# One score pass per unit, a block-diagonal product for the last keys, and one shared pool of PSUM banks in a top-k attention kernel with a feed-forward block

## The chip, the cores and the metric

The kernel runs on one core of a Trainium2 chip. The metric is the device time of one execution in microseconds (us). The kernel before took 1854.19 us, the median of three runs (1853.1 to 1854.46). One more execution was profiled; it took 1853.37 us, and the span from its first to its last instruction is 1851.6 us. Five engines work beside each other: TensorE (PE, with its weight loads shown apart as PEld), VectorE (DVE), ScalarE (ACT), GpSimd (POOL) and SyncE (SP), which issues the transfers.

## The reference

There are 8 batches of 8 heads with 576 positions of 64 numbers. Per head, the scores of all queries against all keys are made, only the 32 largest scores of each query are kept, and a softmax over them weighs the values. The heads are then laid side by side into rows of 512 numbers, and a normalised feed-forward block with a residual follows.

```python
scores = scale * np.matmul(q, k.transpose(0, 1, 3, 2))
kth = np.partition(scores, -top_k, axis=-1)[..., -top_k:-top_k + 1]
scores = np.where(scores >= kth, scores, -1000000000.0)
attn = softmax(scores)                       # over the keys
x = heads_side_by_side(attn @ v)             # (8, 576, 512)
xn = (x - mean(x)) / sqrt(var(x) + 1e-6) * g_ln
out = x + np.maximum(xn @ w_ch1, 0.0) @ w_ch2
```

All inputs come as 64-bit or 32-bit floats, and the kernel computes in 32-bit floats. The feed-forward weights come as 64-bit numbers; the kernel fetches them in 32 pieces and turns them into 32-bit floats itself (class `Piece`).

## The kernel before, in words

**Jobs, units, groups.** A job is a batch and a pair of heads. A unit is one tile of 128 queries of both heads of a job, so it has two score tiles of 128 x 576. A job has four such units and a fifth, the rest unit, whose 64 last queries of both heads share one tile. In batch 0 a job is split in two, so that the first rows are finished early. There are 160 units. Two or three units form a group (`lo_half`, `hi_half`), over which the product with the values is made at once.

**The pipeline.** The main loop (lines 745 to 834) has one step per unit, and the order on each engine is the order in which the code is written. In step n, VectorE searches the 32 largest scores of unit n (`select`, four rounds of MAX8 and MATCH_REPLACE8, lines 358 to 375). TensorE makes the scores of unit n+1 (`scores`), ScalarE copies them from PSUM to `sc`, GpSimd masks unit n-1 (`mask`), ScalarE takes the exponential of unit n-2 (`weigh`), TensorE turns these weights so that keys lie on partitions (`turn`), and for the group whose last unit is n-3, `values` multiplies them with the values and `place` turns the product back and puts it into the rows `x`. `sc` has three buffers, `e` has two.

**The scores.** `scores(u, s)` (lines 330 to 356) makes half s of the keys, 288 columns, for both heads. A head has 64 numbers, so the product of the first head uses rows 0 to 63 of the array and that of the second rows 64 to 127. The two products go to two PSUM banks and are copied by two ScalarE instructions (line 356). The first half is written at the step's start (line 760), the second half behind the first turned tile (line 793).

**The values.** `values(g)` (lines 469 to 484) adds five pairs of products in one bank. In the first four, the values of each head (128 keys, 64 numbers) fill half of the array's columns. In the fifth, the last 64 keys of each head take one quarter of the array each. The number of columns that stream through is 256 for a group of two units and 320 with a rest unit.

**PSUM.** The eight banks are shared out at lines 101 to 103: two for the scores (`scps`), three for turned tiles (`tpps`), three for products (`mmps`: values, turned-back rows `xo`, both feed-forward products and the means of the weights).

**The feed-forward block.** When a batch's rows are finished its block is handed to a list (`give`, line 718), and `fill()`, called eight times in a step, takes products from it by a plan of costs and shares, so each step has a fixed number of feed-forward products at fixed places. A block of four row tiles stands for 20 steps. What is left at the end runs behind the loop. After batches 3 and 7 the block of the collected rest rows comes on top. While the weights are still being converted (the first 18 steps or so), `weights(n, phase)` puts that work between the parts of a step; `mean_of` (line 200) multiplies freshly converted weights on TensorE and is written at a step's end.

Of the kernel before, what the change touches and what calls it, by code (L numbers as in the profile page):

```python
# [11 lines left out]
FP32 = mybir.dt.float32  # L12
U32 = mybir.dt.uint32
PSUM = bass.MemoryType.PSUM
# [6 lines left out]
J = 4  # L21
# [7 lines left out]
def kernel(  # L29
# [34 lines left out]
    nc = tc.nc  # L64
    P = nc.NUM_PARTITIONS
    B, H, S, D = q.shape
# [4 lines left out]
    R = S - JP  # L71
# [6 lines left out]
    def pool(name, bufs, **kw):  # L78
        return ctx.enter_context(tc.tile_pool(name=name, bufs=bufs, **kw))

    GQ = 2 * P + R
    HALF = S // 2

    consts = pool("consts", 1)
    ldpool = pool("ld", 1)
    kqpool = pool("kq", 4)
    vpool = pool("v", 3)
    scpool = pool("sc", 3)
    wpool = pool("wk", 2)
    epool = pool("e", 2)  # L90
# [7 lines left out]
    opool = pool("o", 2)  # L98
    xtpool = pool("xt", 1)
    hpool = pool("h", NF + 2)  # L100
    scps = pool("scps", 2, space=PSUM)
    tpps = pool("tpps", 3, space=PSUM)
    mmps = pool("mmps", 3, space=PSUM)

    def const(shape, name):
        return consts.tile(shape, FP32, tag=name, name=name)

    def turned():
        return tpps.tile([P, 512], FP32, tag="tp", name="tp")

    def product(name):
        return mmps.tile([P, 512], FP32, tag="mm", name=name)

    ident = const([P, P], "ident")
    make_identity(nc, ident[:])
    eps = const([P, 1], "eps")
# [174 lines left out]
            job.ins[name] = t  # L291

    def load_values(job):
        vb = vpool.tile([P, 2 * J + 1, D], FP32, tag="v", name="vb")
        for hh in range(2):
            rows = v[job.b, 2 * job.hp + hh]
            k0, end = (0, JP) if hh == 0 else (R, 0)
            nc.sync.dma_start(
                vb[:, hh * J : (hh + 1) * J, :],
                rows[k0 : k0 + JP, :].rearrange("(c p) d -> p c d", p=P),  # L300
            )
            nc.sync.dma_start(
                vb[hh * R : (hh + 1) * R, 2 * J, :], rows[end : end + R, :]
            )
        job.v = vb

    def turn_heads(job):
        job.T = {}
        for name in "kq":
            job.T[name] = kqpool.tile([P, S], FP32, tag=name + "T", name=name + "T")  # L310
            nc.vector.transpose(job.T[name][:], job.ins[name][:])

    class Unit:
        def __init__(self, job, group, qt):
            self.job, self.group, self.qt = job, group, qt
            self.rest = qt == J
            self.tiles = [(0, 1)] if self.rest else [(0,), (1,)]
            self.sc = None  # L320
            self.shared = False

    class Group:
# [3 lines left out]
            self.units = [Unit(job, self, qt) for qt in qts]  # L327
            self.pt = self.den = None

    def scores(u, s):  # L330

        T = (u.job.twin or u.job).T
        kT, qT = T["k"], T["q"]
        q0 = u.qt * P
        ql = R if u.rest else P
        if u.sc is None:
            u.sc = scpool.tile([P, 2, S], FP32, tag="sc", name="sc")
        pss = [scps.tile([P, 512], FP32, tag="scps", name="scps") for _ in u.tiles]
        for ps, hs in zip(pss, u.tiles):
            for i, hh in enumerate(hs):  # L340
                r = slice(hh * D, (hh + 1) * D)
                parts = [(0, s * HALF, HALF)]
                if u.rest and hh == 1:
                    parts = [(0, R + s * HALF, HALF - s * R)]
                    if s:
                        parts += [(HALF - R, 0, R)]
                for o, k0, width in parts:
                    nc.tensor.matmul(  # L348
                        ps[i * R : i * R + ql, o : o + width],
                        qT[r, q0 : q0 + ql],  # L350
                        kT[r, k0 : k0 + width],
                        start=True,
                        stop=True,
                    )
        for t, ps in enumerate(pss):
            nc.scalar.copy(u.sc[:, t, s * HALF : (s + 1) * HALF], ps[:, 0:HALF])  # L356

    def select(u, i):

# [51 lines left out]
    def turn(u):  # L411

        g = u.group
        if g.pt is None:
            g.pt = ptpool.tile([P, 2 * J + 1, GQ], FP32, tag="pt", name="pt")
        q0 = sum(P for x in g.qts if x < u.qt)
# [51 lines left out]

    def values(g):
        vb = g.job.v  # L470
        av = product("av")
        for c in range(J + 1):
            for h in range(2):
                rows = slice(h * R, (h + 1) * R) if c == J else slice(0, P)
                blk = 2 * J if c == J else h * J + c
                nc.tensor.matmul(  # L476
                    av[h * D : (h + 1) * D, 0 : g.nq],
                    vb[rows, blk, :],
                    g.pt[rows, blk, 0 : g.nq],
                    start=(c == 0),  # L480
                    stop=(c == J),
                )
        g.oT = otpool.tile([P, GQ], FP32, tag="oT", name="oT")
        nc.scalar.copy(g.oT[:, 0 : g.nq], av[:, 0 : g.nq])  # L484
# [9 lines left out]
    def place(g):  # L494

        b, hp = g.job.b, g.job.hp
        for i, qt in enumerate(g.qts):
            if qt == J:
                if b % 2 == 0:
                    oTr[hp] = restpool.tile([P, P], FP32, tag=f"oTr{hp}", name="oTr")  # L500
                r0 = R * (b % 2)
                nc.gpsimd.tensor_copy(
                    oTr[hp][:, r0 : r0 + R], g.oT[:, i * P : i * P + R]
                )
                continue
            if (b, qt) not in xs:
                pair = xpool.tile([P, 2, DM], FP32, tag="x", name="x")
                for j in range(2):
                    xs[b, qt // 2 * 2 + j] = pair[:, j]
            ps = product("xo")  # L510
            nc.tensor.transpose(ps[:, 0:P], g.oT[:, i * P : (i + 1) * P], ident[:])
            put(xs[b, qt], ps, hp * P, g.den, 2 * qt)

    def place_rest(b, hp):
        if hp == 0:
            rs[b // 2] = rpool.tile([P, DM], FP32, tag="r", name="r")[:]
        ps = product("xo")
        nc.tensor.transpose(ps[:, 0:P], oTr[hp][:], ident[:])
        put(rs[b // 2], ps, hp * P, dr[b // 2], 2 * hp)

# [109 lines left out]
    jobs = []  # L630
# [6 lines left out]
    units = []  # L637
# [60 lines left out]
    def at(i):  # L698
        return units[i] if 0 <= i < N else None
# [35 lines left out]
    weights(-2, 0)  # L735
    turn_heads(fresh[0])
    load(fresh[1], nc.sync)
    scores(units[0], 0)
    scores(units[0], 1)
    load_gain()  # L740
    load_values(jobs[0])
    weights(-1, 0)
    weights(-1, 2)
    recips = {}
    for n in range(END):
# [3 lines left out]
        u, nxt, mk, ex = at(n), at(n + 1), at(n - 1), at(n - 2)  # L749
        g = at(n - 3).group if at(n - 3) and at(n - 3).group.last == n - 3 else None  # L750
# [5 lines left out]

        if ex:
            weigh(ex, 0)
        if nxt:
            scores(nxt, 0)  # L760
        if u:
            select(u, 0)
        for den in recips.pop(n, []):
# [6 lines left out]
        if g:  # L770
            values(g)
# [18 lines left out]
        weights(n, 1)  # L790
        fill()
        if nxt:
            scores(nxt, 1)
        fill()
        if g:
            place(g)
# [27 lines left out]
        if g and g.job.hp == NHP - 1:  # L824
            for qt in g.qts:
                if qt < J:
                    blk, i = block_of[g.job.b, qt]
                    blk.stats(i, xs[g.job.b, qt])
        if late and late.job.hp == NHP - 1:
            r = late.job.b // 2  # L830
            blk, i = block_of["r", r]
# [36 lines left out]
```

## Time and profile before

| what | value |
|---|---|
| median of three runs | 1854.19 us |
| profiled execution's own time | 1853.37 us |
| its span | 1851.6 us |
| TensorE busy | 1709.7 us (92%) |
| VectorE busy | 1520.9 us (82%) |
| GpSimd busy | 1210.2 us (65%) |
| ScalarE busy | 942.3 us (51%) |
| mean granted TensorE clock | 0.966 |

Times in the rows below are us from the span's start unless marked ns. A busy share is a mean over stretches that differ much, so the rows give the stretches apart. TensorE's ends are modelled: a matmul's row lasts longer than the time until the next one can start, so the start-to-start distance is what a matmul costs. Every matmul on 32-bit floats has two records in the trace, except the transposes, which have one. A wait in square brackets is the idle time of the engine just before the row, with the one that ended it.

### The profile page before, as it was taken

The numbers are of one execution on the slowest core, as the hardware profiler recorded it, in microseconds if no ns is written. First come the engines' busy times: TensorE is split into PE (matmuls) and PEld (weight loads), VectorE is DVE, ScalarE is ACT, GpSimd is POOL, SyncE is SP. The second block draws the span as 40 slices with busy tenths as digits, with TensorE's granted clock in tenths as the row PEclk, the third lists the DMA queues.
The fourth block names the chain that finished last, engine by engine and source line by source line (L and its number), as shares of the span: only waits on it lengthen the run. The fifth ranks groups of instructions, "written<-read, shape, count | busy, mean of one in ns | idle before, by whom it ended". The sixth has DMA issues, their size and how long they took to land.

```text
span 1851.6 us, 22080 instructions
## 1 busy us (share of the span) xinstructions
PE 1709.7 (92%) x6849; PEld 827.4 (45%) x6849; DVE 1520.9 (82%) x3155; ACT 942.3 (51%) x2430; POOL 1210.2 (65%) x956
## 2 busy tenths in 40 slices
PE   3565998888999999999999999999999999999998
PEld 1223645533444444444444644444444444444455
DVE  7889899999999999999877688999999999960000
ACT  4566956544655465555444546545654565542110
POOL 5878877777777777677565557777777777760000
PEclk9676999999999999999999999999999999999999
DMA  7322221111111011111101011101110110000000
GB/s 185 91 81 64 59 38 24 23 18 26 21 22 24 22 26 20 20 31 31 20 19 25 19 31 20 20 19 32 32 20 19 31 23 16 6 12 6 6 18 11
DMA packets 210429, 57.16 MB, mean 31 GB/s; under 512 B 201604, under 2 KB 201608, under 8 KB 210312
## 3 DMA queue, kind: packets, MB, share of 16 engines
q1 hardware_dynamic: 207936, 55.46, 13.4%
q8 instruction: 54, 0.88, 0.2%
q10 hardware_dynamic: 2376, 0.30, 0.1%
q14 instruction: 63, 0.52, 0.1%
HBM read 46.27 MB, written 9.44 MB: 30 GB/s over the span
## 4 chain that ended last, share of the span: by engine, by line
PE 62%; DVE 14%; issue 11%; POOL 8%; ACT 5%; DMA 0%; POOLq 0%; SPq 0%; DVEq 0%; ACTq 0%
PE hps L574 20%; PE ops L591 19%; PE scps L348 8%; DVE m L366 7%; PE av L476 7%; DVE wk L371 6%; PE tp L421 5%; POOL e L396 2%; POOL w L175 1%; POOL size L174 1%; POOL e L399 1%; POOL e L394 1%; POOL size L165 1%; ACT xT L566 1%; ACT sc L356 1%
## 5 line engine op out<-in xcount | busy, mean ns | idle before, releaser
L396 POOL TENSOR_SCALAR e<-sc,m 128x576 f32<-128x576 f32 x270 | 599.0, 2218 | 287.2 <-PE tp L450 87.1
L366 DVE MAX8 m<-wk 128x8 f32<-128x576 f32 x864 | 612.9, 746 | 1.8
L574 PE MATMUL hps<-xT,w 128*128 128x512 f32 (+1 forms) x1408 | 574.8, 532 | 22.6 <-ACT xT L566 13.7
L591 PE MATMUL ops<-w,h 128*128 128x512 f32 x1152 | 565.2, 609 | 1.8 <-ACT x L488 1.2
L371 DVE MATCH_REPLACE8 wk<-m,wk 128x576 f32<-128x576 f32 x576 | 423.9, 743 | 0.0
L399 POOL TENSOR_TENSOR e<-e,sc 128x576 f32<-128x576 f32 x270 | 380.6, 1410 | 22.5
L356 ACT COPY sc<-scps 128x288 f32<-128x288 f32 x576 | 204.9, 403 | 249.5 <-PE scps L348 170.1
L574 PEld LDWEIGHTS hps<-xT,w 128*128 128x128 f32 x1408 | 241.5, 192 | 190.2 <-issue 147.3
L348 PE MATMUL scps<-kT,qT 64*128 64x288 f32 (+3 forms) x1344 | 255.7, 455 | 28.7 <-ACT sc L356 20.7
L591 PEld LDWEIGHTS ops<-w,h 128*128 128x128 f32 x1152 | 193.3, 191 | 183.8 <-issue 179.3
L366 DVE MAX8 m<-sc 128x8 f32<-128x576 f32 x288 | 203.6, 744 | 68.0 <-ACT sc L356 67.9
L406 ACT ACTIVATE e<-e,bias 128x576 f32<-128x576 f32 x288 | 224.9, 781 | 6.5 <-POOL e L399 5.8
L421 PE MATMUL tp<-ident,e 128*128 128x128 f32 x1152 | 183.3, 283 | 39.7 <-ACT e L406 36.2
L421 PEld LDWEIGHTS tp<-ident,e 128*128 128x128 f32 x1152 | 143.4, 145 | 167.8 <-issue 95.3
L371 DVE MATCH_REPLACE8 wk<-m,sc 128x576 f32<-128x576 f32 x288 | 212.0, 743 | 0.0
L348 PEld LDWEIGHTS scps<-kT,qT 64*128 64x128 f32 (+1 forms) x1344 | 107.3, 180 | 231.6 <-issue 72.3
L433 ACT COPY pt<-tp 128x512 f32<-128x512 f32 x256 | 151.0, 590 | 102.6 <-PE tp L421 101.1
L476 PE MATMUL av<-pt,vb 128*64 128x320 f32 (+3 forms) x1280 | 186.5, 426 | 3.9 <-ACT pt L433 2.4
L586 ACT ACTIVATE h<-hps 128x512 f32<-128x512 f32 (+1 forms) x176 | 92.2, 524 | 131.8 <-PE hps L574 131.5
L601 POOL TENSOR_TENSOR o<-o,x 128x512 f32<-128x512 f32 x32 | 40.8, 1274 | 178.4 <-ACT o L600 178.3
L476 PEld LDWEIGHTS av<-pt,vb 128*64 128x64 f32 (+1 forms) x1280 | 83.2, 139 | 113.5 <-issue 59.4
L484 ACT COPY oT<-av 128x256 f32<-128x256 f32 (+1 forms) x64 | 25.6, 400 | 136.5 <-PE av L476 136.4
(68 smaller groups left out, 959.3 us busy)
## 6 DMA issues: line engine op xcount, KB each, us to landing
raw<-in_moe_w_ch_dram SPq DMA_DIRECT2D x32, 512.0 KB, 3.9
kin<-in_k_dram SPq DMA_DIRECT2D x128, 72.0 KB, 2.4
vb<-in_v_dram SPq DMA_DIRECT2D x72, 128.0 KB, 2.5
qin<-in_q_dram SPq DMA_DIRECT2D x124, 72.0 KB, 2.4
out_dram<-o SPq DMA_DIRECT2D x32, 256.0 KB, 2.1
vb<-in_v_dram SPq DMA_DIRECT2D x72, 16.0 KB, 2.3
dr<-den SPq DMA_DIRECT2D x64, 0.2 KB, 1.7
out_dram<-o SPq DMA_DIRECT2D x8, 128.0 KB, 2.3
```

What stands on the lines that cost most here:

```text
L348: nc.tensor.matmul(ps[i * R : i * R + ql, o : o + width], qT[r, q0 : q0 + ql], kT[r, k0 : k0 + width], start=True, stop=True,)
L356: nc.scalar.copy(u.sc[:, t, s * HALF : (s + 1) * HALF], ps[:, 0:HALF])
L366: nc.vector.max(m[:, t, :], u.cur[t])
L371: nc.vector.match_replace(u.wk[t][:], m[:, t, :], u.cur[t], LOWEST)
L396: nc.gpsimd.tensor_scalar(e, sc, u.thr[:, t, 7:8], MASKED, ALU.is_lt, ALU.mult)
L399: nc.gpsimd.tensor_tensor(e, e, sc, ALU.add)
L406: nc.scalar.activation(u.e[:, t], u.e[:, t], AF.Exp, bias=u.bias[:, t : t + 1], scale=scale, accum_out=g.den[:, col : col + 1],)
L421: nc.tensor.transpose(ps[:, c * P : (c + 1) * P], u.e[:, t, c * P + t * R : (c + 1) * P + t * R], ident[:],)
L433: nc.scalar.copy(g.pt[:, t * J : (t + 1) * J, q0 : q0 + P], ps[:].rearrange("p (c n) -> p c n", n=P),)
L476: nc.tensor.matmul(av[h * D : (h + 1) * D, 0 : g.nq], vb[rows, blk, :], g.pt[rows, blk, 0 : g.nq], start=(c == 0), stop=(c == J),)
L574: nc.tensor.matmul(ps["h"][:, 0:N], w1[:, c, f * P : (f + 1) * P], xT[0][:, c, 0:N], start=(c == 0), stop=(c == NC - 1),)
L591: nc.tensor.matmul(ps["o"][:], hT[f][:, i * P : (i + 1) * P], w2[:, f, :], start=(f == 0), stop=(f == NF - 1),)
```

## The change

Three things change, and the costs and shares of the plan stay as they were.

**Scores in one go.** `scores(u)` makes both halves, four banks' worth, and then issues the four copies. It stands only where the second half stood; the call at the step's start is gone.

**Last keys as one product.** Three constant tiles of 128 x 128, `ends0` to `ends2`, are set to zero once by GpSimd. The transfers of the last 64 keys' values go into two diagonal blocks of one of them, so that one full product of 128 rows and 128 columns does what the fifth pair did. It is now the first product of the sum.

**Banks shared anew.** Scores, turned tiles, the values' product and `xo` take turns in one pool of five banks (`brief`). Three banks remain for the feed-forward products and the means.

```diff
-    scps = pool("scps", 2, space=PSUM)
-    tpps = pool("tpps", 3, space=PSUM)
+    psps = pool("ps", 5, space=PSUM)
     mmps = pool("mmps", 3, space=PSUM)
+    def brief(name):
+        return psps.tile([P, 512], FP32, tag="ps", name=name)
...
+    ends = [const([P, P], f"ends{i}") for i in range(NV)]
+    for t in ends:
+        nc.gpsimd.memset(t[:], 0.0)
...
             nc.sync.dma_start(
-                vb[hh * R : (hh + 1) * R, 2 * J, :], rows[end : end + R, :]
+                job.ends[hh * R : (hh + 1) * R, hh * D : (hh + 1) * D],
+                rows[end : end + R, :],
             )
...
-    def scores(u, s):
+    def scores(u):
+        u.sc = scpool.tile([P, 2, S], FP32, tag="sc", name="sc")
+        made = [score_half(u, s) for s in range(2)]
+        for s, pss in enumerate(made):
+            for t, ps in enumerate(pss):
+                nc.scalar.copy(u.sc[:, t, s * HALF : (s + 1) * HALF], ps[:, 0:HALF])
...
-        av = product("av")
-        for c in range(J + 1):
+        av = brief("av")
+        nc.tensor.matmul(
+            av[:, 0 : g.nq], g.job.ends[:], g.pt[:, 2 * J, 0 : g.nq],
+            start=True, stop=False,
+        )
+        for c in range(J):
             for h in range(2):
...
-        if nxt:
-            scores(nxt, 0)
         if u:
             select(u, 0)
...
         if nxt:
-            scores(nxt, 1)
+            scores(nxt)
```

On TensorE, in the step of a rest unit in a later batch, the order of before is this (scps are scores, av the values' product, tp turned weights, xo the turned-back product, ops a feed-forward product):

```order
L348 MATMUL scps<-kT,qT 128x288 x2
L476 MATMUL av<-pt,vb 64x256 x10
L421 MATMUL tp<-ident,e 128x128 x4
L348 MATMUL scps<-kT,qT 128x288 x2
L511 MATMUL xo<-ident,oT 128x128 x2
L591 MATMUL ops<-w_125,h 128x512
L421 MATMUL tp<-ident,e 128x128 x4
```

The same place in the changed kernel:

```order
L485 MATMUL av<-pt,ends_116 128x256
L491 MATMUL av<-pt,vb 64x256 x8
L434 MATMUL tp<-ident,e 128x128 x4
L362 MATMUL scps<-kT,qT 128x288 x4
L526 MATMUL xo<-ident,oT 128x128 x2
L606 MATMUL ops<-w_128,h 128x512
L434 MATMUL tp<-ident,e 128x128 x4
```

The two products at the step's start moved behind the first turned tile, and the two quarter products of the sum became one full product at its front.

On ScalarE, in the fourth step, while weights are converted, the order of before is this (sc_485 are the next unit's scores, e_500 the mask of the unit before, e_397 the weights of the unit before that):

```order
L406 ACTIVATE e_397,den_380<-e_397,bias_396 128x576
L356 COPY sc_485<-scps_486 128x288
L356 COPY sc_485<-scps_487 128x288
L384 ACTIVATE less_501<-m3_476 128x1
L385 ACTIVATE bias_499<-m0_389 128x2
L386 ACTIVATE e_500<-sc_303,less_501 128x576
```

The same place in the changed kernel:

```order
L419 ACTIVATE e_393,den_383<-e_393,bias_392 128x576
L397 ACTIVATE less_497<-m3_479 128x1
L398 ACTIVATE bias_495<-m0_385 128x2
L399 ACTIVATE e_496<-sc_343,less_497 128x576
L400 ACTIVATE e_496<-e_496 128x576
```

The two copies of scores no longer stand ahead of the four instructions that prepare the mask; they follow later in the step with the other two.

On TensorE, in the same fourth step, before:

```order
L204 MATMUL mean_479<-w1_124,gmat_179 128x512 x4
L348 MATMUL scps_486<-kT_427,qT_429 128x288
L348 MATMUL scps_487<-kT_427,qT_429 128x288
L421 MATMUL tp_519<-ident_117,e_397 128x128 x4
L348 MATMUL scps_536<-kT_427,qT_429 128x288
L348 MATMUL scps_537<-kT_427,qT_429 128x288
```

And in the changed kernel:

```order
L212 MATMUL mean_482<-w1_127,gmat_182 128x512 x4
L434 MATMUL tp_515<-ident_120,e_393 128x128 x4
L362 MATMUL scps_533<-kT_423,qT_425 128x288
L362 MATMUL scps_534<-kT_423,qT_425 128x288
L362 MATMUL scps_537<-kT_423,qT_425 128x288
L362 MATMUL scps_538<-kT_423,qT_425 128x288
```

The turned tile now comes straight behind the mean, and the four score products behind it.

## Rows read from the trace of the kernel before

**Rows 1.** Windows: stretch, length, busy of PE, PEld, DVE, ACT, POOL; clock, DMA.

```profile
0.00:200.00 200.00, 115.34 (x428) 58.58 (x429) 164.83 (x320) 127.01 (x302) 146.20 (x133) 0.76 0.40 102
200.00:500.00 300.00, 262.10 (x1205) 140.61 (x1204) 298.62 (x623) 176.66 (x485) 230.87 (x182) 0.95 0.13 28
500.00:875.00 375.00, 371.52 (x1535) 169.42 (x1534) 359.28 (x753) 200.75 (x524) 280.81 (x217) 1.00 0.13 25
875.00:1121.00 246.00, 243.77 (x980) 122.01 (x980) 186.48 (x386) 114.20 (x292) 143.78 (x109) 1.00 0.11 22
1121.00:1653.00 532.00, 526.66 (x2154) 239.10 (x2153) 506.94 (x1061) 289.74 (x758) 393.14 (x304) 1.00 0.11 21
1653.00:1852.00 199.00, 190.30 (x553) 97.72 (x551) 4.76 (x14) 33.94 (x74) 15.35 (x15) 1.00 0.04 11
```

**Rows 2.** Waits of VectorE, 0 to 200: total us, times, longest.

```profile
DVE m L366 <- ACT sc L356: 11.7, 6, 3.7
DVE den L764 <- POOL den L809: 11.5, 5, 2.7
```

**Rows 3.** Waits of VectorE, 500 to 875.

```profile
DVE st L536 <- ACT x L488: 6.2, 2, 3.1
DVE m L366 <- ACT sc L356: 4.7, 3, 1.8
```

**Rows 4.** Waits of VectorE, 875 to 1121.

```profile
DVE m L366 <- ACT sc L356: 38.8, 11, 8.3
DVE st L536 <- ACT x L488: 13.9, 2, 8.7
```

**Rows 5.** Waits of VectorE, 1121 to 1655.

```profile
DVE m L366 <- ACT sc L356: 12.7, 6, 3.7
DVE st L536 <- ACT x L488: 10.0, 3, 3.9
```

**Rows 6.** Timeline of TensorE around a score burst: start, us, instruction, times.

```profile
882.37 1.02 PE L574 MATMUL hps<-xT,w 128*128 128x512 f32 x2
883.32 0.76 PE L348 MATMUL scps<-kT,qT 64*128 64x288 f32 x4
884.01 2.84 PE L574 MATMUL hps<-xT,w 128*128 128x512 f32 x6
886.69 0.60 PE L421 MATMUL tp<-ident,e 128*128 128x128 f32 x4
887.13 1.88 PE L574 MATMUL hps<-xT,w 128*128 128x512 f32 x4
888.85 0.27 PE L450 MATMUL tp<-ident,e 128*128 128x128 f32 x1
```

**Rows 7.** Timeline of weight loads at the end of one product with the values.

```profile
870.88 0.20 PEld L476 LDWEIGHTS av<-pt,vb 64*64 64x64 f32 x4 [0.38 <-issue]
871.46 0.30 PEld L574 LDWEIGHTS hps<-xT,w 128*128 128x128 f32 x2 [0.38 <-issue]
```

**Rows 8.** Waits of TensorE, 875 to 1121, the longest.

```profile
PE hps L574 <- ACT xT L566: 0.9, 2, 0.7
```

**Rows 9.** Timeline around the end of a rest unit's step.

```profile
767.90 0.76 PE L348 MATMUL scps<-kT,qT 64*128 64x288 f32 x4
...
768.74 0.70 ACT L356 COPY sc<-scps 128x288 f32<-128x288 f32 x2 [1.42 <-PE scps L348]
...
774.19 1.42 DVE L366 MAX8 m<-sc 128x8 f32<-128x576 f32 x2 [1.79 <-ACT sc L356]
```

**Rows 10.** Waits of GpSimd, 20 to 200, the longest.

```profile
POOL e L394 <- ACT e L387: 31.3, 6, 7.7
```

**Rows 11.** Timeline of the fourth step, weights being converted.

```profile
66.25 0.70 ACT L356 COPY sc<-scps 128x288 f32<-128x288 f32 x2 [11.96 <-PE scps L348]
...
68.66 1.41 POOL L394 TENSOR_TENSOR e<-sc,e 128x576 f32<-128x576 f32 x1 [5.88 <-ACT e L387]
...
71.79 1.42 DVE L366 MAX8 m<-sc 128x8 f32<-128x576 f32 x2 [2.79 <-ACT sc L356]
```

More of the change, by code (lines that the diff above doesn't have):

```diff
@@ L79, in pool @@
         return ctx.enter_context(tc.tile_pool(name=name, bufs=bufs, **kw))
+    NV = 3
     GQ = 2 * P + R
@@ L86 @@
     kqpool = pool("kq", 4)
-    vpool = pool("v", 3)
+    vpool = pool("v", NV)
     scpool = pool("sc", 3)
@@ L106, in const @@
         return consts.tile(shape, FP32, tag=name, name=name)
+    def brief(name):
+        return psps.tile([P, 512], FP32, tag="ps", name=name)
     def turned():
-        return tpps.tile([P, 512], FP32, tag="tp", name="tp")
+        return brief("tp")
     def product(name):
         return mmps.tile([P, 512], FP32, tag="mm", name=name)
+    ends = [const([P, P], f"ends{i}") for i in range(NV)]
+    for t in ends:
+        nc.gpsimd.memset(t[:], 0.0)
     ident = const([P, P], "ident")
@@ L293, in load_values @@
     def load_values(job):
-        vb = vpool.tile([P, 2 * J + 1, D], FP32, tag="v", name="vb")
+        vb = vpool.tile([P, 2 * J, D], FP32, tag="v", name="vb")
+        job.ends = ends[jobs.index(job) % NV]
         for hh in range(2):
@@ L319, in __init__ @@
             self.tiles = [(0, 1)] if self.rest else [(0,), (1,)]
-            self.sc = None
             self.shared = False
@@ L328, in __init__, with score_half @@
             self.pt = self.den = None
-    def scores(u, s):
+    def scores(u):
[4 more added lines that the diff above has]
+                nc.scalar.copy(u.sc[:, t, s * HALF : (s + 1) * HALF], ps[:, 0:HALF])
+    def score_half(u, s):
         T = (u.job.twin or u.job).T
@@ L335, in scores @@
         ql = R if u.rest else P
-        if u.sc is None:
-            u.sc = scpool.tile([P, 2, S], FP32, tag="sc", name="sc")
-        pss = [scps.tile([P, 512], FP32, tag="scps", name="scps") for _ in u.tiles]
+        pss = [brief("scps") for _ in u.tiles]
         for ps, hs in zip(pss, u.tiles):
@@ L354, in scores @@
                     )
-        for t, ps in enumerate(pss):
-            nc.scalar.copy(u.sc[:, t, s * HALF : (s + 1) * HALF], ps[:, 0:HALF])
+        return pss
     def select(u, i):
@@ L470, in values @@
         vb = g.job.v
-        av = product("av")
-        for c in range(J + 1):
+        av = brief("av")
[4 more added lines that the diff above has]
+        for c in range(J):
             for h in range(2):
-                rows = slice(h * R, (h + 1) * R) if c == J else slice(0, P)
-                blk = 2 * J if c == J else h * J + c
                 nc.tensor.matmul(
                     av[h * D : (h + 1) * D, 0 : g.nq],
[L478 to L481, printed above, removed]
+                    vb[:, h * J + c, :],
+                    g.pt[:, h * J + c, 0 : g.nq],
+                    start=False,
+                    stop=(c == J - 1),
                 )
@@ L509, in place @@
                     xs[b, qt // 2 * 2 + j] = pair[:, j]
-            ps = product("xo")
+            ps = brief("xo")
             nc.tensor.transpose(ps[:, 0:P], g.oT[:, i * P : (i + 1) * P], ident[:])
@@ L516, in place_rest @@
             rs[b // 2] = rpool.tile([P, DM], FP32, tag="r", name="r")[:]
-        ps = product("xo")
+        ps = brief("xo")
         nc.tensor.transpose(ps[:, 0:P], oTr[hp][:], ident[:])
@@ L737 @@
     load(fresh[1], nc.sync)
-    scores(units[0], 0)
-    scores(units[0], 1)
+    scores(units[0])
     load_gain()
```

## Prediction

> **What bounds the kernel now.** I read the windows first, then the waits of VectorE stretch by stretch, then the timeline at single places. The windows show five stretches of the loop and a tail [rows 1]. From 200 to 500 VectorE is busy 298.6 of 300 us: it alone sets the time. From 500 to 875 and from 1121 to 1653 TensorE (371.5 of 375, 526.7 of 532) and VectorE (359.3 of 375, 506.9 of 532) are both nearly full. From 875 to 1121, where batch 3's rows and the first rest rows are multiplied in the same twenty steps, TensorE is full and VectorE stands for 59 us. Behind 1653 TensorE works off what is left. From 0 to 200 no engine is full; GpSimd leads ScalarE there while weights are converted.
>
> The loop can't become shorter than VectorE's own work, which the change leaves alone, so its waits are the most that can be won: 23.2 us in two groups before 200 [rows 2], none from 200 to 500, 10.9 from 500 to 875 [rows 3], 52.7 of the 59 from 875 to 1121 [rows 4], 22.7 from 1121 on [rows 5]. Nearly all are for score copies or for the copy of turned-back rows `x`. So the question is how far TensorE, which feeds both, gets ahead.
>
> **Scores in one go: the price of a burst.** Four records of feed-forward products in a row, with full-array work ahead and behind, take 888.85 - 887.13 = 1.72 us, 0.43 each [rows 6]. The pair of score products between takes 884.01 - 883.32 = 0.69. Its 4 records of 288 columns run two at a time, one head in each half of the rows, so streaming alone is 2 x 288/512 x 0.43 = 0.48: 0.21 over. The product before it takes 0.95 where two records cost 0.86: 0.09 over. The six records behind it take 2.68 where 2.58 is due: 0.10 over. A burst thus costs 0.40 beside its streaming, at its two ends, where the array changes from full to half rows and back. The merged burst should stream 0.96 and pay the 0.40 once, so TensorE saves 0.40 in each unit, if four products follow each other without a hole.
>
> The Trainium skill speaks against this term: "TensorE: Matmul & The Clock Gate", Part 3, Measured speedup vs the span model, gives packed products a span of one product plus about 4 ns per tile. By that rule a pair lasts 0.48 to 0.49, merging saves nothing, and this term is 0. The trace disagrees with 0.69 between the starts, so I go by the row; the page leaves out the ends.
>
> **Last keys as one product.** The quarter products stand from 870.88 to 871.46, 0.58 us for 256 columns [rows 7]; two records of 256 columns of full array cost 0.43. As the first of the sum the full product needs no change of shape against the feed-forward product ahead, so a group saves 0.15; bounds are 0 (the change out of the half columns may cost what the quarters' did) and 0.25 (it may be cheaper). GpSimd's three fills of zeros lie in its first, idle microseconds. The transfers keep their number and size.
>
> **Banks.** Five banks in turn serve a step's 7 tenants, or 9 to 10 with a group. A tenant waits for the copy of the one five places ahead. In a step with a group the last score product waits for the copy of `av`, the two `xo` for the copy of the turned tile and of the first scores. I take 0.3 us of new TensorE wait in such a step, two of them in five. The bounds are 0 and 1.4 in every unit, the four copies of 0.35 [rows 9] all in the open.
>
> **What each stretch makes of it.** Five units and two groups, a job, save TensorE 5 x 0.40 + 2 x 0.15 - 2 x 0.3 = 1.7 us; with no bank waits 2.3.
>
> *875 to 1121.* TensorE waits for nothing worth telling, 0.9 us at most for one releaser [rows 8], so its saving counts in full: 20 units are four jobs, 4 x 1.7 = 7, or 9 where the many feed-forward products between hide the bank waits. TensorE also comes in with a lead it didn't have, some 1 to 4 us. I take 10, between 7 and 14.
>
> *500 to 875.* 38 units save TensorE 13 to 17 us, more than the 10.9 VectorE waits. The waits stand at the end of rest units, whose search is half as long while TensorE's step is not. At 774.19 VectorE had waited 1.79 [rows 9]. In that step alone the burst of 767.90 leaves (0.69 and its outer 0.19) and `av` shortens by 0.15, so the merged burst starts 1.03 earlier. The first score tile is then complete with the third copy, not the first: two copies at 0.30 later, 0.6. The net is 0.4 earlier. The four steps ahead add 0.3 to 0.4 each, so the wait closes. I take 9, between 6 and 11.
>
> *1121 to 1653.* 22.7 us, of which the last 3.9 belong to the last rows and stay. TensorE comes out of the full stretch with no lead and builds it at 1 to 2 us a job, so the first waits stay in part. I take 15, between 8 and 19.
>
> *200 to 500 and the tail.* Nothing: VectorE is full in the one, and the tail's products stay the same.
>
> *0 to 200.* After a mean, TensorE waits for converted weights, the first score products stand behind it, and ScalarE waits 11.96 us for them with the next mask's preparation queued behind the copy; so GpSimd, otherwise without a pause, waits 5.88, and VectorE 2.79 [rows 11]. Such waits of GpSimd come to 31.3 us in six [rows 10]. In the new order nothing that waits for TensorE's scores stands ahead of these four ScalarE instructions, and GpSimd can go on at once. Late next are the four score copies themselves, behind the mean, the turned tile and a burst at the lower clock (granted 0.76 in this stretch). Of VectorE's 23.2 us some 8 come before the second search or after the conversion. I take 9, between 2 and 15.
>
> The sum is 10 + 9 + 15 + 9 = 43 us: from the profiled execution's 1853.4 to 1810, and 0.8 more against the median, 1811. The ends add up to 23 and 59, that is 1831 and 1795.
>
> **The rivals.**
>
> *The copies, not TensorE, are what VectorE waits for.* At rest units ScalarE has the exponential, a turned tile's copy and now four score copies in a row ahead of the search. For it: the first score tile is whole two copies later. Against it: at 768.74 ScalarE itself had stood 1.42 us for TensorE [rows 9], and it is busy only 55% from 1121 on [rows 1]. Then only the full stretch and half of the early term remain, 9 + 4: 1841.
>
> *Slower: the ring of five makes TensorE wait for ScalarE.* With the next turned tile behind the scores' banks, a late copy stops TensorE, feed-forward products included, since its order is fixed. Beyond 0.46 us in each unit (2.3 over five) the saving is gone. At 0.8 us, half of four copies and one half-ready tile, a unit costs 0.35 more; over the 38 + 20 + 55 units from 500 on this is 40 us, less the early 4: 1890. Against it: the old pools, with two score banks, give no such wait among those of TensorE [rows 8].
>
> By the Trainium skill, "TensorEngine Tiling (Array Packing)", PSUM Bottleneck, packing speeds up TensorE but not the copying out of PSUM, which may become the bound. No row here shows that bound; by the page this rival would be the likelier one.
>
> *The change doesn't do what it says.* If a burst of four has a hole where the second pair starts, it costs two bursts. Some 7 us, most of them of the early term, are left at best, since the score tile comes later in the step: 1847, or as before.
>
> **How the numbers follow.** The forecast has a chance of 0.70, the copies 0.15, the slower case 0.08, the change without effect 0.07. The range reaches from 1794 past the forecast's own 1831 to the copies' case, 1840; about 0.2 stays outside, mostly the slower case and the change without effect. A measurement tells 0.2%, 3.7 us, from no change. Faster: 0.70 + 0.14 + 0.02 = 0.86. Within 0.2%: 0.05. Slower: 0.09.
>
> **What would show it.** Score bursts of 8 records should stand about 1.17 us from their start to the next product, once a unit; no quarter products remain, and the full product is followed without a hole. VectorE's waits for `sc` from 500 to 875 should be under 2 us, and the twenty full steps shorter by 7 to 14. GpSimd's 5.88 us waits behind the means should be gone. I am wrong if TensorE's waits for ScalarE's copies of `sc`, `oT` or `pt` come to more than some 25 us in the loop, if VectorE still waits at rest units with TensorE ahead, or if TensorE's clock falls from 1.00 behind 500 because it now stands more.

## The result, and the profile after

The changed kernel takes 1784.7 us (median of four runs, 1783.71 to 1785.47), the kernel before 1853.93 us on the same chip (four runs, 1853.1 to 1854.46). The ratio is 0.9627, with a 95% interval of 0.961 to 0.9643. The profiled execution took 1784.44 us, with a span of 1782.5 us, 69.1 less than before. The forecast was 1811 in 1794 to 1840: the direction was right, the gain too small by 26 us and the range too high.

| | before | after |
|---|---|---|
| TensorE busy | 1709.7 us | 1642.9 us |
| VectorE busy | 1520.9 us | 1517.1 us |
| GpSimd busy | 1210.2 us | 1209.0 us |
| mean granted TensorE clock | 0.966 | 0.971 |

To see where the time went, I take the moment at which VectorE starts the search of the same unit in both traces. The kernel before starts it at 255.66 us for unit 20 (the first of batch 1), 489.24 for unit 45, 867.03 for unit 84, 1121.92 for unit 105 and 1643.63 for the last, 159. The last four stand near borders of [rows 1]; unit 20 stands in the stretch where VectorE is full. The table gives each kernel's start minus that of before; E1 to E9 are the experiments below.

| us against before | unit 20 | 45 | 84 | 105 | 159 | end of span |
|---|---|---|---|---|---|---|
| changed kernel | -23.4 | -23.4 | -34.9 | -48.3 | -66.2 | -69.1 |
| E1 two products apart, copies together | -25.0 | -25.0 | -26.2 | -27.1 | -28.1 | -29.4 |
| E2 before, call moved, old banks | -13.2 | -13.2 | +7.9 | +20.5 | +54.3 | +54.0 |
| E3 changed, two calls | -1.5 | -1.5 | -2.2 | -4.5 | -7.6 | -8.9 |
| E4 changed, quarter products | -24.0 | -24.0 | -35.6 | -45.6 | -60.7 | -63.1 |
| E5 changed, a full product between | -23.7 | -23.7 | -20.4 | -19.9 | -13.5 | -14.4 |
| E6 before, new banks | -0.6 | -0.6 | -2.5 | -3.5 | -4.8 | -5.6 |
| E7 before, copies behind the mask | -12.8 | -12.8 | -13.4 | -13.4 | -13.4 | -13.4 |
| E8 before, copies behind the conversion | -21.6 | -21.6 | -20.9 | -20.9 | -21.0 | -21.0 |
| E9 changed, scores next to the values (second run) | -23.1 | -23.1 | -34.6 | -49.5 | -69.4 | -74.2 |

So the changed kernel wins 23.4 us up to unit 20, nothing up to 45, then 11.5, 13.3 and 17.9, and 2.9 in the tail. The forecast had 9, 0, 9, 10, 15 and 0. The windows of the changed kernel, laid so that they begin and end near the same work as those of [rows 1], the first border 12 us later (columns as there):

```profile
0.00:189.29 189.29, 121.57 (x470) 69.37 (x471) 175.26 (x343) 138.92 (x335) 157.32 (x144) 0.81 0.44 113
189.29:476.60 287.31, 239.29 (x1132) 136.89 (x1130) 285.96 (x601) 165.23 (x451) 220.06 (x173) 0.95 0.13 26
476.60:840.10 363.50, 357.48 (x1513) 179.37 (x1512) 361.88 (x762) 202.28 (x537) 281.46 (x218) 1.00 0.13 26
840.10:1072.70 232.60, 229.95 (x946) 124.18 (x944) 182.84 (x378) 108.50 (x280) 141.34 (x108) 1.00 0.11 23
1072.70:1586.80 514.10, 507.43 (x2126) 253.75 (x2127) 508.00 (x1065) 289.51 (x764) 394.13 (x305) 1.00 0.11 22
```

VectorE now fills its windows from 476.6 to 840.1 (361.88 of 363.5) and from 1072.7 to 1586.8 (508.00 of 514.1); before it had 359.3 of 375 and 506.9 of 532. In the full stretch TensorE is busy 229.95 of 232.6 us, before 243.8 of 246, for nearly the same work: it alone sets the pace there, and a faster one. TensorE's mean granted clock stayed at 1.00 from 476.6 on.

The first window ends where unit 15's search starts. The same work in the kernel before takes 22.58 us more:

```profile
0.00:211.87 211.87, 126.50 (x485) 66.01 (x485) 176.67 (x343) 138.80 (x336) 156.80 (x141) 0.77 0.39 101
```

VectorE's work differs by 1.4 us, GpSimd's by 0.5; the rest of the difference is waiting. TensorE's mean granted clock rose from 0.77 to 0.81, but that is not what wins: over the same work E6 has 0.79 and gains 0.6 us, and E4, with 0.84, is only 0.6 us ahead of the changed kernel. GpSimd's waits of the changed kernel there (us in total, times, longest), against the 31.3 us of [rows 10]:

```profile
POOL e L407 <- ACT e L400: 8.9, 4, 6.4
```

VectorE's waits there, after the first load:

```profile
DVE m L379 <- ACT sc L345: 3.3, 2, 2.8
DVE size L176 <- POOL size L173: 2.3, 2, 1.4
DVE den L776 <- POOL den L821: 1.5, 1, 1.5
```

GpSimd waits 22.4 us less for the mask's preparation, as much as the whole gain. Four of its waits in the kernel before stand behind the means, 22.6 us together: the 5.88 at 68.66 of [rows 11] and these.

```profile
39.27 1.42 POOL L394 TENSOR_TENSOR e<-sc,e 128x576 f32<-128x576 f32 x1 [4.97 <-ACT e L387]
...
98.25 1.42 POOL L394 TENSOR_TENSOR e<-sc,e 128x576 f32<-128x576 f32 x1 [5.88 <-ACT e L387]
...
127.98 1.41 POOL L394 TENSOR_TENSOR e<-sc,e 128x576 f32<-128x576 f32 x1 [5.88 <-ACT e L387]
```

In those four steps the changed kernel's GpSimd doesn't wait for the mask at all. Of its 8.9 us 6.4 are what is left of the longest wait of before, 7.7 us, which stands behind no mean. VectorE's waits fell by nearly as much, from 28.4 us (the 23.2 of [rows 2] and three smaller ones, below) to 7.1:

```profile
DVE rstd L546 <- ACT rstd L540: 3.1, 1, 3.1
DVE size L168 <- POOL size L165: 1.3, 2, 0.8
DVE w L215 <- PE mean L204: 0.8, 2, 0.5
```

These three rows are of the kernel before, 0 to 211.87. From 40 us on VectorE is now busy 146.9 of 149.3 us (before, 148.4 of 171.9), so the stretch has become VectorE's, and little more could be won in it. In the fourth step, which [rows 11] shows of before, ScalarE of the changed kernel does this:

```profile
53.28 0.68 ACT L400 ACTIVATE e<-e 128x576 f32<-128x576 f32 x1
...
60.20 0.59 ACT L446 COPY pt<-tp 128x512 f32<-128x512 f32 x1 [3.80 <-PE tp L434]
```

and GpSimd this:

```profile
57.14 1.41 POOL L407 TENSOR_TENSOR e<-sc,e 128x576 f32<-128x576 f32 x1
```

The mask is prepared (53.28) three microseconds before GpSimd is free to use it (57.14, no wait in brackets; 5.88 before), and ScalarE's wait for TensorE now stands behind it, where it holds up nothing that GpSimd needs. It is 3.80 us instead of 11.96.

TensorE around one product with the values and one burst of scores:

```profile
829.57 0.59 PE L485 MATMUL av<-pt,ends 128*128 128x256 f32 x2
830.10 1.95 PE L491 MATMUL av<-pt,vb 128*64 128x256 f32 x16
831.98 1.12 PE L589 MATMUL hps<-xT,w 128*128 128x512 f32 x2
832.94 0.60 PE L434 MATMUL tp<-ident,e 128*128 128x128 f32 x4
833.47 1.24 PE L362 MATMUL scps<-kT,qT 64*128 64x288 f32 x8
834.64 1.13 PE L589 MATMUL hps<-xT,w 128*128 128x512 f32 x2
835.60 0.27 PE L526 MATMUL xo<-ident,oT 128*128 128x128 f32 x1
836.35 0.33 PE L526 MATMUL xo<-ident,oT 128*128 128x128 f32 x1 [0.47 <-ACT sc L345]
```

The burst of eight records takes 834.64 - 833.47 = 1.17 us, as worked out; the two products of [rows 6] would take 1.38 and pay their ends twice. The second `xo` waits 0.47 us for a copy of scores five banks ahead. Such waits from 476 to 1585:

```profile
PE xo L526 <- ACT sc L345: 4.4, 5, 1.2
```

Of VectorE's waits, those of [rows 3] are gone: it has none from 476 to 851. In the full stretch, 840 to 1073, these two answer to [rows 4]:

```profile
DVE m L379 <- ACT sc L345: 32.6, 10, 7.8
DVE st L551 <- ACT x L503: 12.0, 2, 8.2
```

and from 1073 to 1585 these to [rows 5] (the 3.9 us for the last rows that are in those are 1.1 us now):

```profile
DVE st L551 <- ACT x L503: 1.6, 2, 1.1
DVE m L379 <- ACT sc L345: 1.3, 1, 1.3
```

That wait for the last rows, first before and then after, lies behind the start of unit 159:

```profile
1653.25 0.69 DVE L536 BATCH_NORM_STATS2 st<-x 128x6 f32<-128x512 f32 x1 [3.85 <-ACT x L488]
...
1584.28 0.69 DVE L551 BATCH_NORM_STATS2 st<-x 128x6 f32<-128x512 f32 x1 [1.12 <-ACT x L503]
```

It is 2.7 us shorter, and that is nearly all of the 2.9 us in the tail. TensorE turns these rows back 8.8 us after unit 159's search begins in the kernel before (1652.39) and 5.9 us after it now (1583.42): its shorter steps in the loop brought it closer to VectorE.

### The profile page after: what moved, and what is told of

It is laid out like the page before. It is cut to its first block, busy times and chain, and to the rows that moved or that the text cites. A ratio compares the mean times of both kernels' runs of the same rounds, so it can differ in the third digit from the quotient of the medians.

```text
span 1782.5 us, 21600 instructions
## 1 busy us (share of the span) xinstructions
PE 1642.9 (92%) x6721; PEld 860.0 (48%) x6721; DVE 1517.1 (85%) x3155; ACT 937.0 (53%) x2430; POOL 1209.0 (68%) x959
## 4 chain that ended last, share of the span: by engine, by line
PE 53%; DVE 29%; issue 11%; ACT 5%; POOL 1%; DMA 1%; ACTq 0%; POOLq 0%; SPq 0%; DVEq 0%
PE hps L589 19%; PE ops L606 16%; DVE m L379 14%; DVE wk L384 12%; PE scps L362 6%; PE av L491 5%; PE tp L434 4%; PE av L485 1%; DVE size L176 1%; ACT e L419 1%; DVE w L223 1%; PE xo L526 1%; POOL o L616 0%; PE tp L463 0%; DVE st L551 0%
## 5 line engine op out<-in xcount | busy, mean ns | idle before, releaser
L589 PE MATMUL hps<-xT,w 128*128 128x512 f32 (+1 forms) x1408 | 555.2, 525 | 12.6 <-ACT xT L581 12.6
L606 PE MATMUL ops<-w,h 128*128 128x512 f32 x1152 | 549.2, 602 | 0.0
L412 POOL TENSOR_TENSOR e<-e,sc 128x576 f32<-128x576 f32 x270 | 381.0, 1411 | 22.6
L589 PEld LDWEIGHTS hps<-xT,w 128*128 128x128 f32 x1408 | 246.9, 192 | 174.6 <-issue 148.6
L606 PEld LDWEIGHTS ops<-w,h 128*128 128x128 f32 x1152 | 197.3, 191 | 184.6 <-issue 183.0
L345 ACT COPY sc<-scps 128x288 f32<-128x288 f32 x576 | 192.0, 413 | 92.1 <-PE scps L362 88.4
L362 PE MATMUL scps<-kT,qT 64*128 64x288 f32 (+3 forms) x1344 | 213.3, 434 | 13.2 <-DVE qT L321 8.0
L362 PEld LDWEIGHTS scps<-kT,qT 64*128 64x128 f32 (+1 forms) x1344 | 119.1, 183 | 132.2 <-issue 54.7
L491 PE MATMUL av<-pt,vb 128*64 128x320 f32 (+1 forms) x1024 | 143.5, 424 | 0.0
L491 PEld LDWEIGHTS av<-pt,vb 128*64 128x64 f32 x1024 | 69.8, 141 | 65.7 <-issue 28.6
```

Of the source, the lines that this page charges most:

```text
L362: nc.tensor.matmul(ps[i * R : i * R + ql, o : o + width], qT[r, q0 : q0 + ql], kT[r, k0 : k0 + width], start=True, stop=True,)
L412: nc.gpsimd.tensor_tensor(e, e, sc, ALU.add)
L491: nc.tensor.matmul(av[h * D : (h + 1) * D, 0 : g.nq], vb[:, h * J + c, :], g.pt[:, h * J + c, 0 : g.nq], start=False, stop=(c == J - 1),)
L589: nc.tensor.matmul(ps["h"][:, 0:N], w1[:, c, f * P : (f + 1) * P], xT[0][:, c, 0:N], start=(c == 0), stop=(c == NC - 1),)
L606: nc.tensor.matmul(ps["o"][:], hT[f][:, i * P : (i + 1) * P], w2[:, f, :], start=(f == 0), stop=(f == NF - 1),)
```

## The experiments

**E1. Score products apart, copies together.** The changed kernel, but the first half's products go back to the step's start; all four copies stay late. `scores_start` makes the first half's products; `scores_end` copies them, makes the second half's and copies those. Banks and last keys stay new.

```diff
+        if nxt:
+            scores_start(nxt)
...
         if nxt:
-            scores(nxt)
+            scores_end(nxt)
```

> The changed kernel, but the products of the first half of the keys stand at the step's start again; their copies stay late, just ahead of the second half's products. TensorE's order is that of before, ScalarE's that of after. Theory (the first 190 us were won because no score copy stands ahead of the mask's preparation on ScalarE): unit 20 starts 18 to 24 us earlier than in the kernel before, as in the changed one; from 500 on the two bursts cost TensorE its 0.40 us a unit again, so nearly all of the later 45 us is lost: 1825 to 1835. Rival (they were won because TensorE makes all scores in one burst, behind the turned tile): unit 20 starts within 6 us of before: 1845 to 1855.

Measured: 1825.76 us (1823.36 to 1827.54), ratio 0.9848 (0.9834 to 0.9863). The whole early gain is there (-25.0 at unit 20) without the merged burst; from unit 45 on only 3 us of 43 are left. TensorE's waits don't explain that: from 480 to 1600 they come to 13.8 us, in the changed kernel to 16.1. Two bursts stand in each step again, 0.68 and 0.69 us:

```profile
1192.67 0.76 PE L368 MATMUL scps<-kT,qT 64*128 64x288 f32 x4
1193.35 1.98 PE L612 MATMUL ops<-w,h 128*128 128x512 f32 x4
...
1196.56 0.76 PE L368 MATMUL scps<-kT,qT 64*128 64x288 f32 x4
1197.25 1.13 PE L612 MATMUL ops<-w,h 128*128 128x512 f32 x2
```

So the early gain comes from the place of ScalarE's copies, the later one mostly from TensorE's single burst.

**E2. The call moved, the old banks.** The kernel before; only the first half's call moves down to the second.

```diff
-        if nxt:
-            scores(nxt, 0)
         if u:
             select(u, 0)
...
         if nxt:
+            scores(nxt, 0)
             scores(nxt, 1)
```

> The kernel before with its two, three and three banks and its quarter products; only the call for the first half is moved down to the second's. Theory: the first 190 us are won (about 20 us), but the second pair of products has to wait for the copies of the first, which stand on ScalarE behind an exponential and a turned tile's copy, 0.5 to 1 us a unit on a TensorE that is full, so from 500 on it is 20 to 60 us slower than before: 1850 to 1890. Rival (the place in the step is what counts, the banks are not): 1790 to 1805.

Measured: 1907.02 us (1904.07 to 1914.04), ratio 1.0294 (1.0269 to 1.0319): the direction was right, the price higher than my range, and the early gain, 13.2 us at unit 20, smaller than the 20 that I gave. TensorE's waits from 300 to 1700, and one such place:

```profile
PE scps L348 <- ACT sc L356: 69.2, 106, 3.2
```

```profile
522.51 0.76 PE L348 MATMUL scps<-kT,qT 64*128 64x288 f32 x4
523.75 1.05 PE L348 MATMUL scps<-kT,qT 64*128 64x288 f32 x4 [0.48 <-ACT sc L356]
```

With two banks the second pair waits for the copies of the first, and the burst (522.51 to 524.73) takes 2.2 us instead of 1.17. The Trainium skill, "TensorEngine Tiling (Array Packing)", PSUM Bottleneck, says that the copying out of PSUM may become the bound of packed products; this run agrees in so far as TensorE waits 69.2 us for copies. But ScalarE is busy only 561.9 of the 1120 us from 480 to 1600, so the bound here is the number of banks, not the speed of copying: in the changed kernel, with five, 4.4 us of waits for score copies are left.

**E3. The changed kernel with two calls.** Banks and last keys stay; products and copies of each half stand where they stood before.

```diff
-    def scores(u):
-        made = [score_half(u, s) for s in range(2)]
...
+    def scores(u, s):
...
+        for t, ps in enumerate(score_half(u, s)):
...
+        if nxt:
+            scores(nxt, 0)
...
-            scores(nxt)
+            scores(nxt, 1)
```

> The changed kernel with two score calls, products and copies, at the places of before; five shared banks and the full product for the last keys stay. Theory: both the early gain and the gain of the single burst go; the full product saves TensorE 0.15 us a group: 1845 to 1853. Rival (the shared banks gave a good part): 1800 to 1830.

Measured: 1844.49 us (1843.39 to 1846.48), ratio 0.9951 (0.9937 to 0.9966), just below the range that I gave. The early gain is gone but for 1.5 us, and GpSimd's old wait is back (0 to 210):

```profile
POOL e L406 <- ACT e L399: 30.3, 6, 6.3
```

Banks and last keys alone are thus worth 8.9 us of span.

**E4. Quarter products again.** The changed kernel, with two products of 64 rows and 64 columns in place of the full one, at the same place.

```diff
-        nc.tensor.matmul(
-            av[:, 0 : g.nq], g.job.ends[:], g.pt[:, 2 * J, 0 : g.nq],
-            start=True, stop=False,
-        )
+        for h in range(2):
+            rows = slice(h * R, (h + 1) * R)
+            nc.tensor.matmul(
+                av[h * D : (h + 1) * D, 0 : g.nq],
+                g.job.ends[rows, h * D : (h + 1) * D],
+                g.pt[rows, 2 * J, 0 : g.nq],
+                start=True,
+                stop=False,
+            )
```

> The changed kernel, but the last keys of each head are two quarter products again, now at the front of the sum. Theory (0.15 us a group on TensorE, which counts only where TensorE is full): the twenty full steps 1 to 1.5 us longer, 1 to 4 us in all: 1786 to 1789. Rival (the full product saves nothing that the end sees, or the last keys' transfers did it): within 1 us of after, 1785.

Measured: 1790.85 us (1790.45 to 1793.05), ratio 0.966 (0.9648 to 0.9673): 6 us above the changed kernel, more than expected.

```profile
887.96 3.60 PE L594 MATMUL hps<-xT,w 128*128 128x512 f32 x8
891.48 0.65 PE L487 MATMUL av<-pt,ends 64*64 64x256 f32 x4
892.06 1.95 PE L496 MATMUL av<-pt,vb 128*64 128x256 f32 x16
```

The quarters take 0.58 us and cost the product ahead of them 0.08 (eight records in 3.52 us, 3.44 due). In the changed kernel the full product takes 0.53 (829.57 to 830.10). The difference of 0.13 per group is the 0.15 forecast; 46 groups stand behind unit 45, so 6 us is what it should come to.

**E5. A full product between the halves.** The changed kernel, with one product of 32 columns on the full array between the two score pairs; its result is not used.

```diff
-        made = [score_half(u, s) for s in range(2)]
+        made = [score_half(u, 0)]
+        nc.tensor.matmul(
+            made[0][0][:, 480:512], ident[:], ident[:, 0:32], start=True, stop=True
+        )
+        made.append(score_half(u, 1))
```

> The changed kernel with one more tiny product of the full array (32 columns, into unused columns of a score bank; its result is not used) between the two halves of the scores: the array changes its shape twice more in each unit, 0.40 us, at unchanged places and order. Theory (from 500 on TensorE's changes of shape were what was saved): the first 190 us as after; the twenty full steps 8 to 9 us longer, and VectorE's waits at rest units return in part: 1804 to 1818. Rival (what counted is where the scores stand in the step): within 3 us of after, 1785.

Measured: 1840.39 us (1838.94 to 1842.02), ratio 0.9928 (0.9913 to 0.9943). It goes the way expected, but costs 56 us, far beyond the range that I gave.

```profile
852.46 0.76 PE L366 MATMUL scps<-kT,qT 64*128 64x288 f32 x4
853.15 0.30 PEld L343 LDWEIGHTS scps<-ident 128*128 128x128 f32 x2 [0.39 <-issue]
853.15 0.41 PE L343 MATMUL scps<-ident 128*128 128x32 f32 x2
853.49 0.76 PE L366 MATMUL scps<-kT,qT 64*128 64x288 f32 x4
854.17 1.12 PE L593 MATMUL hps<-xT,w 128*128 128x512 f32 x2
```

From 852.46 to 854.17 the burst takes 1.71 us instead of 1.17. The product between streams 2 x 32 columns, 0.05 us by the 0.43 of 512; so 0.49 of the 0.54 come beside it. The two changes of shape would make 0.40 of that by [rows 6]; the rest may be the inserted product's own weight loads (0.30 us from 853.15), which no run tells apart. Over the 115 units from 45 on 0.54 makes 62 us, of which 55 arrived by the end of the span. TensorE's waits did not rise. The early gain is untouched (-23.7). The Trainium skill, "TensorE: Matmul & The Clock Gate", Part 3, Measured speedup vs the span model, gives packed products a span of one product plus about 4 ns per tile. That rule has no term for a full product between two packed pairs, which cost 0.49 us beside its streaming here.

**E6. The banks alone.** The kernel before, with five banks in turn and three.

```diff
-    scps = pool("scps", 2, space=PSUM)
-    tpps = pool("tpps", 3, space=PSUM)
+    psps = pool("ps", 5, space=PSUM)
...
-        av = product("av")
+        av = brief("av")
```

> The kernel before with only the banks shared anew, five and three. Theory (the shared banks by themselves win little): 1850 to 1855, nothing in the first 190 us. Rival (the 9 us that two calls on the new banks won are the banks'): 1844 to 1847.

Measured: 1850.02 us (seven runs, 1847.35 to 1851.91), ratio 0.9975 (0.9965 to 0.9985): a small gain, most of it from unit 45 on (the execution in the table took 1847.75). I had forecast a small loss for the banks.

**E7. Copies behind the mask's preparation.** The kernel before; TensorE, banks and last keys as they were. Only the first half's two copies move, behind the mask's preparation and its first part.

```diff
-            scores(nxt, 0)
+            scores(nxt, 0, hold=True)
...
         if mk:
             prepare(mk)
             mask(mk, 0)
+        if nxt:
+            copies(nxt, 0)
         weights(n, 0)
```

> The kernel before, all products and banks as they were; only the two copies of the first half stand behind the preparation and the first part of the mask in each step, still ahead of the weights' conversion. Theory (GpSimd, not VectorE, bounded the first 190 us, and its waits came from ScalarE's four preparing instructions held behind a copy): GpSimd's waits for the mask's preparation fall from 31 to under 14 us, and unit 20 starts earlier by as much, 12 to 22 us; the rest as before: 1832 to 1842. Rival (the weights' conversion and the exponential behind the copy matter as much, so all of ScalarE's order has to move): under 10 us, 1844 to 1850.

Measured: 1839.91 us (1839.61 to 1840.39), ratio 0.9923 (0.991 to 0.9936). It brings 12.8 of the 23.4 us, and 0.6 later. GpSimd's waits, 0 to 200, where the search of unit 15 starts:

```profile
POOL size L165 <- ACT size L160: 17.3, 7, 3.5
...
POOL e L399 <- ACT e L392: 5.6, 3, 4.7
```

The wait for the mask fell from 31.3 to 5.6, but GpSimd now waits for the conversion: its three ScalarE instructions (L160 to L164) stand behind the waiting copies now (3.6 us of such waits before).

**E8. Copies behind the conversion too.** As E7, with the copies one place further down.

```diff
+        weights(n, 0)
         if nxt:
             copies(nxt, 0)
-        weights(n, 0)
```

> The kernel before; only the copies of the first half's scores move, as in the run with the copies behind the mask, but one place further: behind the mask preparation, the first mask part and the three ScalarE instructions of the weights' conversion. TensorE, banks and the last keys are those of before. Theory (the early gain is GpSimd's backlog, held up by ScalarE instructions queued behind a copy that waits for TensorE; half of it is the mask's preparation, the other half the conversion's instructions): the unit that follows the conversion starts 20 to 25 us earlier, GpSimd's waits for the conversion (16.2 us in six when only the mask stood ahead) shrink to under 6, and the rest of the loop is as before: 1828 to 1834. Rival (the other half comes from TensorE's merged burst or from the shared banks): the conversion's place changes nothing, 1838 to 1842 again.

Measured: 1834.35 us (1832.41 to 1834.81), ratio 0.9889 (0.9875 to 0.9902), just above the range that I gave. At unit 16 it stands at -22.1, the changed kernel at -22.6. GpSimd's waits, 0 to 189.75, where the search of unit 15 starts:

```profile
POOL e L399 <- ACT e L392: 9.2, 4, 6.7
...
POOL size L165 <- ACT size L160: 3.4, 3, 1.3
```

The order of two copies on ScalarE, with not one instruction of TensorE moved, makes the early gain: at unit 20, 12.8 us by the mask and 8.8 more by the conversion. It adds up with E3 in total, 21.0 + 8.9 = 29.9, where E1, which has both, has 29.4; place by place it does so less well (at unit 45 23.1 and 25.0).

**E9. Scores next to the values' product.** The changed kernel; from the twentieth step on, in a step with a group, the scores stand directly ahead of the product with the values, and the full product comes last in its sum.

```diff
+        close = g and nxt and n > 18
+        if close:
+            scores(nxt)
         if g:
             values(g)
...
-        if nxt:
+        if nxt and not close:
             scores(nxt)
```

> The changed kernel; from the 20th step on, in a step with a group, the four score products stand directly ahead of the values' product, and the full product for the last keys comes last in its sum. One change of the array's shape goes in each group, 0.2 us. Theory (changes of shape are what TensorE's full steps pay): the twenty full steps 1.5 us shorter, 1 to 4 us in all: 1781 to 1784. Rival (the copies of the scores now stand ahead of the copy of the values' product on ScalarE, and TensorE waits for that): 1785 to 1795.

Measured: 1780.24 us, ratio 0.9599 (0.9586 to 0.9611), a little more than expected. The changed kernel had been timed on another occasion, so both ran once more, one after the other on one chip.

> The changed kernel once more, unchanged, as the measure for the other run of this call: 1783 to 1786.

> The version with the scores directly ahead of the values' product once more, beside the changed kernel on the same chip. Theory (one more change of the array's shape goes where two half-column and half-row products stand side by side; a group's step saves about 0.1 to 0.2 us): 3 to 5 us below the changed kernel, 1779 to 1782. Rival (the difference seen before lies between two chips): no difference beyond 1.5 us.

Measured: the changed kernel 1784.15 us (1783.79 to 1785.27), ratio 0.9621 (0.9608 to 0.9634); the new version 1779.23 us (1779.05 to 1780.48), ratio 0.9596 (0.9583 to 0.9609). It beats the changed kernel by 4.9 us, and the two sets of runs don't overlap.

```profile
888.70 1.24 PE L362 MATMUL scps<-kT,qT 64*128 64x288 f32 x8
889.87 1.95 PE L487 MATMUL av<-pt,vb 128*64 128x256 f32 x16
891.75 0.70 PE L494 MATMUL av<-pt,ends 128*128 128x256 f32 x2
892.28 1.02 PE L589 MATMUL hps<-xT,w 128*128 128x512 f32 x2
893.14 0.38 PE L434 MATMUL tp<-ident,e 128*128 128x128 f32 x2
```

Burst, product and full product take as long as in the changed kernel (1.17, 1.88, 0.53). But no feed-forward pair behind them pays: in the changed kernel the pair after the product and the pair after the burst last 0.96 us each (831.98 and 834.64), here the one pair lasts 0.86. That is 0.20 per group, at most 11 us over the 56 groups of batches 1 to 7. Where VectorE sets the pace nothing of it arrives: at unit 84 this version stands at -34.6, the changed kernel at -34.9.

## Why the prediction was wrong in its size

**The step that failed is the early term.** "Of VectorE's 23.2 us some 8 come before the second search or after the conversion. I take 9, between 2 and 15." Measured: 23.4. That is 14.4 of the 26 us that the forecast missed; 8.7 lie in the three stretches behind unit 45 and 2.9 in the tail. The mechanism was the one described: a score copy that waits for TensorE stood ahead of the mask's preparation in ScalarE's queue, and GpSimd waited. The size was wrong for three reasons.

- I discounted VectorE's waits: 8 us struck out, three fifths of the other 15 taken. In fact 4.8 of the 23.2 us are left, and 7.1 of the 28.4. The row to go by was GpSimd's own wait, with VectorE's whole 28.4 us as the cap. Before unit 15's search GpSimd waited 34.9 us for the mask's preparation and the conversion (31.3 and 3.6), and what went of that is what unit 15 gained, within 0.8 us in each run: 22.8 and 22.6 in the changed kernel, 24.5 and 24.2 in E1, 18.5 and 17.8 in E2, 0.7 and 1.5 in E3, 12.0 and 11.8 in E7, 22.3 and 22.1 in E8.
- I followed only the mask behind the waiting copy. E7 and E8 show that the conversion's three ScalarE instructions behind it, which GpSimd waits for as well, are worth 9 us.
- I set "late next" (the four copies behind mean, turned tile and burst) against the gain. VectorE waits only 3.3 us for them after all, 2.8 of it at the very first search: the next search needs them later than GpSimd needs its inputs.

**TensorE's three terms had the right mechanism and came out too small**: 9, 10 and 15 forecast, 11.5, 13.3 and 17.9 measured, the first 0.5 beyond its upper end. The burst of 1.17 us and the full product (0.13 per group by E4) are as worked out. What was mis-sized are the bank waits, 0.3 us in each step with a group, about 14 us from 500 on. E6 gives a gain of 4 us in place of a loss, and the changed kernel's `xo` waits come to 4.4. A likely reason, which no run isolates, is that `av` and `xo` no longer take banks from the feed-forward products.

**Nothing from 200 to 500** held: -23.4 at both ends. **The tail** was to bring nothing and brought 2.9 us. The prediction let the 3.9 us for the last rows stay; they fell to 1.1, because TensorE's shorter work brought it closer to VectorE. E8, with TensorE's work as before, keeps 3.9 us there and gains nothing.

**The rivals.** That VectorE waits for the copies at rest units fell: no wait is left from 476 to 851. The slower case, the ring of five, fell too, yet E2 shows that it was priced in earnest: with two banks the same move costs 53 us. That the burst has a hole fell with the 1.17 us. That merging saves nothing, with a pair of 0.48 to 0.49 us, fell with E1's pairs of 0.68 and 0.69; that figure took a product's bare streaming for its whole duration.

## What to carry to other kernels

On an engine that works strictly in its written order, look for instructions that wait for a slow producer and list all that is queued behind them, for every engine that waits for those; here moving two copies by some places was worth 20 us. Price it by the whole idle time of the engine that these instructions feed, and take the idle time of the next engine behind it as the cap. On TensorE put products that use the array in the same shape next to each other, across stages too, and give them enough PSUM banks to run through.

## What the runs showed of the hardware

A change of the array's shape has a price of its own: a full product of 32 columns put into a score burst cost 0.49 us beside the 0.05 that it streams (E5; 0.40 of it is what the two changes cost by [rows 6]), and a score burst right ahead of a product with the values saved 0.20 us (E9), although the two use different halves of the array (64 rows by 128 columns, 128 rows by 64): from one kind of half to the other costs less than by way of the full array. So a small full-array product is no cheap filler between packed ones.
